# Attention, a gated MLP and a second MLP after layer norm: the norm's factor per token is moved from the second MLP's input to its output

## The chip, the cores and the metric

The kernel runs on one core of one Trainium2 chip. The metric is the device time of the whole program in microseconds (us); lower is better.

## What is computed

Two sequences of 3136 tokens, 256 features, float32 throughout. Cut to what matters:

```python
scores = z @ z.T / S;  x = u * (np.maximum(scores, 0) ** 2 @ v)          # attention, gated by u
h = np.maximum(x @ w_in, 0)                                              # MLP 1, 256 -> 1024
conv = sum(conv_w[k] * shifted(h, k - 1) for k in range(3))              # along the tokens
y = (h * sigmoid(conv)) @ w_out                                          # 1024 -> 256
mu = y.mean(-1, keepdims=True);  var = ((y - mu) ** 2).mean(-1, keepdims=True)
xn = (y - mu) / np.sqrt(var + 1e-6) * g_ln                               # layer norm
out = y + np.maximum(xn @ w_ch1, 0) @ w_ch2                              # MLP 2 and residual
```

## The kernel before, in words

Every float32 product is split into a high and a low part, so that each matrix product is three matmuls on TensorE (PE): high by high, low by high, high by low. Names ending in `h` and `l` are these parts.

Attention runs over 14 chunks of up to 512 tokens; its outputs grow in the PSUM tile `av` and go through DRAM (`gated`) to the MLPs. The MLPs run over 17 blocks of tokens, 15 of three tiles of 128 tokens and two of two tiles, in `mlps(c, when)` (L811). The work of attention for later chunks stands between that of the MLPs. Only the last three blocks have no attention left beside them.

Inside a block, for each of eight slices of the 1024 hidden features: `up` makes hidden values (`hps`, L831 to L833), ScalarE (ACT) and VectorE (DVE) apply relu, convolution and sigmoid and split the result into `gh` and `gl`, and `down` (L847 to L849) adds tile after tile into the accumulator `y`, a PSUM tile of two banks: tiles 0 and 1 lie in the first bank, tile 2 in the second. There is one place for `y`, so the first MLP's output, the second MLP's output and the next block's first MLP follow each other in it. (For the last two blocks the first MLP's accumulator is `av`, the second's a shared `y`, one half each.)

When the first MLP is complete, ACT copies all tiles of the accumulator to SBUF (`ysb`, L932). DVE takes statistics per tile from the copy (`bst`, L937), aggregates them to mean and variance (`mv`, L942) and adds epsilon (`ve`, L949); GpSimd (POOL) raises that to the power −1/2 (`rs`, L953); a Newton step on DVE sharpens it (L960 to L962); DVE writes `xn`, centred and scaled, per tile (L972). PE transposes `xn` into `tps` (L992); ACT and DVE multiply by g and split into `xth` (L1000) and `xtl` (L1005). The second MLP follows: `h2ps`, `g2h` (L1020), `g2l` (L1025), `down` again. At the end one DVE operation adds the accumulator to `ysb` (residual, L1033), and one DMA on SyncE's queue stores the block (L1039).

The order of everything is set ahead of time by a planner (`Program.order`, L154): each operation has the engines it may run on with a price in us, what it reads and writes (by tile of the accumulator), and a due time, `when` or `when2`, from a few constants (`TURN`, `DEFER`). On each engine, among those ready, the earliest due goes first, and the instructions of each engine are then held to that order. The waits on semaphores between engines are not the planner's: they follow from which tile buffers each instruction reads and writes. Where the planner leaves a gap on PE, `fill` (L1136, L1138) puts matmuls on zeros into it, if the accumulator last written has more to come.

The few lines on which this hangs:

```python
key = (o.ways[0][0] != e, o.due, o.n)                # L219: what goes first on engine e
n = int((gaps.get(o, 0.0) - 0.1) / FILL)             # zero matmuls in a planned gap
if n > 0 and not y_used:
    fill(n, wps, True)
elif n > 0 and to_come[last[0]]:
    fill(n, last[1](), False)
```

Of the kernel before, what the change touches and what calls it, by code (L numbers as in the profile page):

```python
# [11 lines left out]
AF = mybir.ActivationFunctionType  # L12
# [3 lines left out]
P = 128  # L16
# [16 lines left out]

UP1, DOWN1, TURN, UP2 = 0.4, 0.14, 0.6, 0.36
LENGTH = 14.0, 14.0, 8.0, 8.0
DEFER = 50.0, 40.0, 0.0
HELP = 1.3
A_PLACES = 4
GH = ("DVE", "ACT")
AH = ("ACT", "DVE")  # L40
CAPS = {"s": 3, "m": 3, "ld": 4}
FUSED = 2, 4, 1
FLOAT = ("ACT", "POOL")
WH = ("ACT", "POOL")
VH = ("ACT", "POOL")
# [45 lines left out]
class Program:  # L91
# [7 lines left out]
    def op(self, ways, fn, reads=(), writes=(), adds=(), takes=(), due=None, late=None, name="", port=False, kb=None):  # L99


        o = Op()
        o.ways, o.fn, o.due, o.late, o.name, o.port, o.kb = ways, fn, due, late, name, port, kb
        o.before, o.after, o.n = set(), [], len(self.ops)
        o.adds, o.spare = tuple(adds), None
        for k in reads:
            assert k in self.writers, (name, k)
            o.before.update(self.writers[k])
            self.readers.setdefault(k, []).append(o)
        for k in writes:  # L110
            o.before.update(self.writers.get(k, ()))
            o.before.update(self.readers.pop(k, ()))
            self.writers[k] = [o]
        for k in adds:
            o.before.update(self.readers.get(k, ()))
            self.writers.setdefault(k, []).append(o)
        o.before.discard(o)
        bufs = []
        for k in (*reads, *writes, *adds, *((t,) for t in takes)):
            if isinstance(k[0], Buf) and k[0] not in bufs:  # L120
                bufs.append(k[0])
        for b in bufs:
            b.users.append(o)
        o.bufs = bufs
        self.ops.append(o)
        return o
# [168 lines left out]
def attn_moe_kernel(ctx: ExitStack, tc: tile.TileContext, zt, ut, v, w_in, conv_w, w_out, g_ln, w1, w2, out):  # L295
# [515 lines left out]
    def mlps(c, when):  # L811
# [115 lines left out]
        def rows(i):  # L927
            return at(y)[:, (i0 + i) * D : (i0 + i + 1) * D]

        op(  # L930
            [("ACT", 0.1 + 0.00078 * n * 2)],
            lambda e: nc.scalar.copy(flat(at(y, "ysb")), flat(at(acc).rearrange("p a b -> p (a b)"))),  # L932
            reads=[(acc, i0 + i) for i in range(ntt)], writes=[(y, i0)], name="ysb",
        )
        for i in range(ntt):
            op(
                [("DVE", 0.328)], lambda e, i=i: nc.vector.bn_stats(at(bst, "bst")[:, i, :], rows(i)),  # L937
                reads=[(y, i0)], writes=[(bst, i)], name="bn",
            )
        for i in range(ntt):  # L940
            op(
                [("DVE", 0.16)], lambda e, i=i: nc.vector.bn_aggr(at(mv, "mv")[:, i, :], at(bst)[:, i, :]),  # L942
                reads=[(bst, i)], writes=[(mv, i)], name="bn",
            )
        def stat():
            return at(ve, "ve")[:, :ntt], at(r, "rs")[:, :ntt], at(q, "rq")[:, :ntt]

        op(
            [("DVE", 0.07)], lambda e: nc.vector.tensor_scalar(stat()[0], at(mv)[:, :ntt, 1], EPS, None, ALU.add),  # L949
            reads=[(mv, i) for i in range(ntt)], writes=[(ve, 0)], name="ve",  # L950
        )
        op(
            [("POOL", 1.285)], lambda e: nc.gpsimd.tensor_tensor(stat()[1], stat()[0], mhalf[:, :ntt], ALU.pow),  # L953
            reads=[(ve, 0)], writes=[(r, 0)], name="pow", port=True,
        )


        def newton(e):
            v_, r_, q_ = stat()
# [2 lines left out]
            nc.vector.scalar_tensor_tensor(r_, q_, 1.5, r_, ALU.add, ALU.mult)  # L962

        op(
            [("DVE", 0.6)], newton, reads=[(ve, 0), (r, 0)], writes=[(r, 1)], takes=[q], name="newton",
        )
        xns = []
        for i in range(ntt):
            xn = buf("xn")
            op(  # L970
                [("DVE", 0.402)],
                lambda e, i=i, xn=xn: nc.vector.tensor_scalar(  # L972
                    at(xn, "xn"), rows(i), at(mv)[:, i, 0:1], at(r)[:, i : i + 1], ALU.subtract, ALU.mult
                ),
                reads=[(y, i0), (mv, i), (r, 1)], writes=[(xn, 0)], name="xn", port=True,
            )
            xns.append(xn)
        if c == NK - 1:
            th, tl = buf("xh", True), buf("xl", True)
        elif tail:  # L980
# [32 lines left out]
        for k in range(NF):  # L1013
            ps = buf("w", kind="m")
            gh, gl = buf("gh", True), buf("gl", True)
            for ways, fn, reads, due, d in up(ps, "w1", k, th, tl, n, when2(TURN + 0.02 + UP2 * k / NF)):
# [21 lines left out]
        dma(  # L1038
            lambda: nc.sync.dma_start(  # L1039
                out=out[s:e_, :].rearrange("(i p) d -> p i d", p=P),  # L1040
                in_=flat(at(y)).rearrange("p (i d) -> p i d", d=D),
            ),
            n, reads=[(y, i0)], due=when2(1.1), name="out",
        )


    def note(*keys):
# [164 lines left out]
```

## Time and profile before

| | |
|---|---|
| median of 3 runs | 1109.61 us (1109.04 to 1109.82) |
| the profiled execution | 1108.97 us |
| its span in the trace | 1107.2 us |
| PE busy | 1093.4 us (99%) |
| DVE busy | 863.4 us (78%) |
| ACT busy | 705.2 us (64%) |
| POOL busy | 31.4 us (3%) |
| clock granted to TensorE, mean | 1.0 |

The span is the part of the execution that the profiler's records cover; the execution's own time is 1.8 us longer. Busy time counts each engine's instructions. Matmuls overlap in the pipeline, so that their recorded lengths add up to more than the time from one start to the next, and a PE that is busy in the table is not PE at its peak: the zero matmuls count as busy too. Before each instruction the trace gives the idle time of its engine and what ended it.

### The profile page before, as it was taken

The page shows a single profiled execution, that of the slowest core. Times are in us where ns is not written, and L with a number is a line of the kernel's source. Part 1 is how long each engine was busy: PE and PEld are TensorE (multiplying, and loading weights), DVE is VectorE, ACT ScalarE, POOL GpSimd, SP SyncE. Part 2 cuts the span into 40 slices and gives each one's busy share as a digit, 9 for nine tenths or more (in the row PEclk, how much of TensorE's full clock was granted, in tenths as well). Part 3 has the DMA queues.
Part 4 walks back from the last instruction along what each step waited for, and adds up shares of the span by engine and source line. Part 5 has one row for each costly group of instructions (what it writes and reads, how often), then busy time and mean ns, then how long its engine had stood idle before and what let it go on. Part 6 is the DMA issues. An engine that isn't in the chain of part 4 may idle for free.

```text
span 1107.2 us, 19228 instructions
## 1 busy us (share of the span) xinstructions
PE 1093.4 (99%) x6674; PEld 1027.3 (93%) x6674; DVE 863.4 (78%) x1828; ACT 705.2 (64%) x1452; POOL 31.4 (3%) x46
## 2 busy tenths in 40 slices
PE   9999999999999999999999999999999999999998
PEld 7777988989999989899989999999899999999998
DVE  7999999987868695969594959595948768478773
ACT  7778887775647575857484857574737547356552
POOL 2000000000000000000000000000000000000000
PEclk9999999999999999999999999999999999999999
DMA  6876887777655431313131413322525635440000
GB/s 201 243 191 156 204 186 175 169 152 161 112 134 89 110 94 43 91 53 94 51 106 46 126 37 79 88 63 58 105 78 97 143 66 97 109 78 27 25 15 20
DMA packets 373778, 115.44 MB, mean 104 GB/s; under 512 B 277296, under 2 KB 365360, under 8 KB 373680
## 3 DMA queue, kind: packets, MB, share of 16 engines
q1 hardware_dynamic: 373680, 114.21, 43.5%
q8 instruction: 52, 0.85, 0.3%
q14 instruction: 46, 0.38, 0.1%
HBM read 64.74 MB, written 46.47 MB: 100 GB/s over the span
## 4 chain that ended last, share of the span: by engine, by line
PE 87%; DVE 4%; DMA 3%; ACT 3%; SPq 2%; issue 1%; POOL 0%; DVEq 0%; ACTq 0%
PE av L746 11%; PE av L749 11%; PE av L748 11%; PE y L847 8%; PE y L849 8%; PE y L848 8%; PE h2ps L831 4%; PE h2ps L832 4%; PE h2ps L833 4%; PE hps L831 4%; PE hps L832 4%; PE hps L833 4%; PE s L704 3%; PE s L705 3%; DMA land<-turned 2%; SPq L651 1%
## 5 line engine op out<-in xcount | busy, mean ns | idle before, releaser
L746 PE MATMUL av<-ah,vh 128*128 128x512 f32 (+2 forms) x700 | 258.6, 369 | 3.2 <-ACT a L722 1.1
L749 PE MATMUL av<-ah,vl 128*128 128x512 f32 (+2 forms) x700 | 256.3, 366 | 0.0
L748 PE MATMUL av<-al,vh 128*128 128x384 f32 (+2 forms) x672 | 247.6, 368 | 2.5 <-DVE al L683 2.0
L1025 DVE SCALAR_TENSOR_TENSOR g2l<-h2ps,g2h 128x384 fp32r<-128x384 f32 (+1 forms) x136 | 73.4, 540 | 114.4 <-ACT g2h L1020 113.4
L1020 ACT ACTIVATE g2h<-h2ps 128x384 fp32r<-128x384 f32 (+1 forms) x136 | 65.3, 480 | 138.8 <-PE h2ps L833 138.1
L746 PEld LDWEIGHTS av<-ah,vh 128*128 128x128 f32 x700 | 131.8, 188 | 17.0 <-ACT ah L394 2.5
L749 PEld LDWEIGHTS av<-ah,vl 128*128 128x128 f32 x700 | 131.7, 188 | 14.3
L748 PEld LDWEIGHTS av<-al,vh 128*128 128x128 f32 x672 | 126.6, 188 | 16.6 <-DVE al L683 6.1
L713 ACT ACTIVATE a<-s 128x512 f32<-128x512 f32 (+2 forms) x196 | 106.2, 557 | 38.2 <-PE s L705 37.6
L683 DVE TENSOR_TENSOR al<-a,ah 128x512 fp32r<-128x512 f32 (+2 forms) x182 | 115.3, 641 | 3.1 <-ACT ah L394 2.1
L683 DVE TENSOR_TENSOR al<-land,ah 128x384 fp32r<-128x384 f32 (+2 forms) x154 | 91.7, 596 | 25.3 <-ACT ah L394 20.9
L847 PE MATMUL y<-woh,gh 128*128 128x256 f32 x392 | 109.9, 280 | 1.1 <-DVE ysb L1033 1.1
L847 PE MATMUL y<-w2h,g2h 128*128 128x256 f32 x392 | 110.0, 281 | 0.2 <-DVE ysb L1033 0.2
L849 PE MATMUL y<-woh,gl 128*128 128x256 f32 x392 | 110.0, 281 | 0.1
L849 PE MATMUL y<-w2h,g2l 128*128 128x256 f32 x392 | 110.0, 281 | 0.0
L848 PE MATMUL y<-w2l,g2h 128*128 128x256 f32 x392 | 109.8, 280 | 0.0
L848 PE MATMUL y<-wol,gh 128*128 128x256 f32 x392 | 109.6, 280 | 0.0
L394 ACT CAST ah<-a 128x512 fp32r<-128x512 f32 (+2 forms) x184 | 105.9, 584 | 4.1 <-PE av L749 1.7
L722 ACT ACTIVATE a<-a 128x512 f32<-128x512 f32 (+2 forms) x183 | 106.8, 594 | 1.6
L626 DVE STREAM_TRANSPOSE bl<-a 128x512 f32<-128x512 f32 (+1 forms) x146 | 94.7, 657 | 9.8 <-ACT a L722 9.2
L394 ACT CAST ah<-land 128x384 fp32r<-128x384 f32 (+2 forms) x136 | 73.8, 546 | 34.7 <-DMA land<-turned 16.7
L882 DVE SCALAR_TENSOR_TENSOR t<-h,cw,t 128x384 f32<-128x384 f32 (+1 forms) x136 | 80.7, 598 | 14.6 <-ACT t L873 14.1
(119 smaller groups left out, 2448.1 us busy)
## 6 DMA issues: line engine op xcount, KB each, us to landing
turned<-bl SPq DMA_DIRECT2D x90, 256.0 KB, 2.5
land<-turned SPq DMA_DIRECT2D x328, 48.0 KB, 2.3
land<-turned SPq DMA_DIRECT2D x168, 56.0 KB, 2.3
turned<-bl SPq DMA_DIRECT2D x44, 192.0 KB, 2.3
land<-turned SPq DMA_DIRECT2D x120, 64.0 KB, 2.5
out_dram<-ysb SPq DMA_DIRECT2D x15, 384.0 KB, 2.7
vst<-in_v_dram SPq DMA_DIRECT2D x11, 512.0 KB, 4.8
x<-gated SPq DMA_DIRECT2D x14, 386.0 KB, 3.9
```

The source lines that it names most:

```text
L394: nc.scalar.copy(dst, src)
L626: [("DVE", price("dve_turn", w))], lambda e: nc.vector.transpose(at(b, "bl")[:, :w], at(ab)[:, :w]),
L683: lambda e: nc.vector.tensor_tensor(at(al, "al")[:, :n], a(), f(at(ah)[:, :n]), ALU.subtract),
L713: [("ACT", price("act_ps", n))], lambda e: nc.scalar.activation(a(), at(ps)[:, :n], AF.Relu),
L722: op([("ACT", price("act", n))], lambda e: nc.scalar.activation(a(), a(), AF.Square), writes=[(ab, 0)], name="square")
L746: nc.tensor.matmul(p, vhj, at(ah)[:, :n], start=first(b, d), stop=False, **kw)
L748: nc.tensor.matmul(p, vhj, at(al)[:, :n], start=False, stop=False, **kw)
L749: nc.tensor.matmul(p, vlj, at(ah)[:, :n], start=False, stop=False, **kw)
L831: nc.tensor.matmul(p, a, h_, start=d == 0, stop=False)
L847: nc.tensor.matmul(p, a, wh, start=first(acc, (i0 + i) // 2), stop=False, **kw)
L848: nc.tensor.matmul(p, a, wl, start=False, stop=False, **kw)
L849: nc.tensor.matmul(p, b, wh, start=False, stop=k == NF - 1, **kw)
```

## The change

The layer norm's factor per token, r, is positive and the second MLP is relu between two linear maps, so r can multiply its output in place of its input. The statistics then read the accumulator in PSUM per tile (L937), and the centred tile is taken from PSUM too, on ACT or DVE (`center`, L951 and L953), with its sign turned (mu − y on ACT is one operation); g is multiplied by −1 once for that (L1085). The copy `ysb` (L962) comes after these in the program, and is now needed by the residual alone. `ve`, power and Newton get due times of their own (`REST`). The residual is a DVE operation per tile, y2 · r + ysb (L1043). The last block's store is two DMAs of one tile each (L1051). `DEFER` for the third last block goes from 50 to 10, so that its second MLP is due earlier. Line numbers in the new kernel's rows are its own: L847 to L849 become L849 to L851, the transposes L1001, fill L1150.

```diff
-DEFER = 50.0, 40.0, 0.0
+DEFER = 10.0, 40.0, 0.0
+CENTER = ("ACT", "DVE")
+REST = 0.9
...
+        def sums1(i, acc=acc):
+            return at(acc).rearrange("p a b -> p (a b)")[:, (i0 + i) * D : (i0 + i + 1) * D]
+
+        for i in range(ntt):
+            op(
+                [("DVE", 0.35)], lambda e, i=i: nc.vector.bn_stats(at(bst, "bst")[:, i, :], sums1(i)),
+                reads=[(acc, i0 + i)], writes=[(bst, i)], name="bn",
+            )
+            op(
+                [("DVE", 0.16)], lambda e, i=i: nc.vector.bn_aggr(at(mv, "mv")[:, i, :], at(bst)[:, i, :]),
+                reads=[(bst, i)], writes=[(mv, i)], name="bn",
+            )
+        xns = []
+        for i in range(ntt):
+            xn = buf("xn")
+
+            def center(e, i=i, xn=xn):
+                mu = at(mv)[:, i, 0:1]
+                if e == "ACT":
+                    nc.scalar.activation(at(xn, "xn"), sums1(i), AF.Identity, bias=mu, scale=-1.0)
+                else:
+                    nc.vector.tensor_scalar(at(xn, "xn"), sums1(i), mu, -1.0, ALU.subtract, ALU.mult)
+
+            op(
+                [(e, price("act_scale" if e == "ACT" else "dve_ps", D)) for e in CENTER], center,
+                reads=[(acc, i0 + i), (mv, i)], writes=[(xn, 0)], name="center",
+            )
+            xns.append(xn)
         op(
             [("ACT", 0.1 + 0.00078 * n * 2)],
             lambda e: nc.scalar.copy(flat(at(y, "ysb")), flat(at(acc).rearrange("p a b -> p (a b)"))),
-            reads=[(acc, i0 + i) for i in range(ntt)], writes=[(y, i0)], name="ysb",
-        )
-        for i in range(ntt):
-            op(
-                [("DVE", 0.328)], lambda e, i=i: nc.vector.bn_stats(at(bst, "bst")[:, i, :], rows(i)),
-                reads=[(y, i0)], writes=[(bst, i)], name="bn",
-            )
...
-            reads=[(mv, i) for i in range(ntt)], writes=[(ve, 0)], name="ve",
+            reads=[(mv, i) for i in range(ntt)], writes=[(ve, 0)], due=when2(REST), name="ve",
...
-            op(
-                [("DVE", 0.402)],
-                lambda e, i=i, xn=xn: nc.vector.tensor_scalar(
-                    at(xn, "xn"), rows(i), at(mv)[:, i, 0:1], at(r)[:, i : i + 1], ALU.subtract, ALU.mult
-                ),
-                reads=[(y, i0), (mv, i), (r, 1)], writes=[(xn, 0)], name="xn", port=True,
-            )
...
-        op(
-            [("DVE", 0.1 + 0.001 * n * 2)],
-            lambda e: nc.vector.tensor_tensor(
-                flat(at(y)), flat(at(acc2).rearrange("p a b -> p (a b)")), flat(at(y)), ALU.add
-            ),
-            reads=[(acc2, i0 + i) for i in range(ntt)], writes=[(y, i0)], name="residual",
-        )
...
+        for i in range(ntt):
+            op(
+                [("DVE", price("dve_3", D))],
+                lambda e, i=i: nc.vector.scalar_tensor_tensor(
+                    rows(i), sums1(i, acc2), at(r)[:, i : i + 1], rows(i), ALU.mult, ALU.add
+                ),
+                reads=[(acc2, i0 + i), (r, 1)], writes=[(y, i0 + i)], name="residual",
+            )
+        for a, b in ((0, 1), (1, ntt)) if c == NK - 1 else ((0, ntt),):
...
+    op([("DVE", 0.07)], lambda e: nc.vector.tensor_scalar(gt, gt, -1.0, None, ALU.mult), writes=[("gt",)], name="gt")
```

Since the planner orders everything anew, the diff doesn't show how instructions move. Three places do, as each engine's list of instructions has them (line, operation, output <- inputs, tile; in brackets what it waits for; x3 counts equal ones).

First place: PE at the end of the second MLP of the fourth block, the last of the eight slices, three tiles of three matmuls. Before:

```order
L847 MATMUL y<-w2h,g2h 128x256 [waits Activation_49]
L848 MATMUL y<-w2l,g2h 128x256
L849 MATMUL y<-w2h,g2l 128x256 [waits DVE_49]
L847 MATMUL y<-w2h,g2h 128x256
L848 MATMUL y<-w2l,g2h 128x256
L849 MATMUL y<-w2h,g2l 128x256
L847 MATMUL y<-w2h,g2h 128x256
L848 MATMUL y<-w2l,g2h 128x256
L849 MATMUL y<-w2h,g2l 128x256
L704 MATMUL s<-hl 128x512
```

After:

```order
L849 MATMUL y<-w2h,g2h 128x256 [waits Activation_49]
L850 MATMUL y<-w2l,g2h 128x256
L851 MATMUL y<-w2h,g2l 128x256 [waits DVE_49]
L849 MATMUL y<-w2h,g2h 128x256
L850 MATMUL y<-w2l,g2h 128x256
L851 MATMUL y<-w2h,g2l 128x256
L849 MATMUL y<-w2h,g2h 128x256 [waits DVE_49]
L850 MATMUL y<-w2l,g2h 128x256
L851 MATMUL y<-w2h,g2l 128x256
L748 MATMUL av<-ah,vh 128x512
```

The third tile's first matmul has gained a wait for DVE. On DVE at the same place the list after reads:

```order
L1034 SCALAR_TENSOR_TENSOR g2l<-h2ps,g2h 128x384 [waits Activation_49] x4
L400 CAST gh<-t 128x384 [waits DVE_49,PE_49]
L1043 SCALAR_TENSOR_TENSOR ysb<-y,rs,ysb 128x256 [waits PE_49]
L915 TENSOR_TENSOR gl<-t,gh 128x384 [waits DVE_49]
L1043 SCALAR_TENSOR_TENSOR ysb<-y,rs,ysb 128x256 [waits PE_49]
L1043 SCALAR_TENSOR_TENSOR ysb<-y,rs,ysb 128x256
L915 TENSOR_TENSOR gl<-t,gh 128x384 [waits Activation_49]
```

Three residuals stand where one of 768 columns stood. The first waits for PE's last matmul on tile 1, the second for PE's on tile 2.

Second place: DVE between the end of the first MLP of the sixth block and its statistics. Before:

```order
L683 TENSOR_TENSOR al<-a,ah 128x512 [waits DVE_49]
L937 BN_STATS bst<-ysb 128x6 [waits Activation_49]
L937 BN_STATS bst<-ysb 128x6 x2
L942 BN_AGGR mv<-bst 128x2 [waits DVE_49] x3
L683 TENSOR_TENSOR al<-land,ah 128x512
L949 TENSOR_SCALAR ve<-mv 128x3 [waits DVE_49]
```

After:

```order
L685 TENSOR_TENSOR al<-a,ah 128x512 [waits Activation_49]
L937 BN_STATS bst<-y 128x6 [waits PE_49]
L937 BN_STATS bst<-y 128x6
L937 BN_STATS bst<-y 128x6 [waits Activation_49]
L941 BN_AGGR mv<-bst 128x2 [waits DVE_49] x3
L685 TENSOR_TENSOR al<-a,ah 128x512
L685 TENSOR_TENSOR al<-land,ah 128x512 [waits DMAHW2_49,DMAHW1_49,DMAHW3_49,DMAHW0_49,Activation_49]
```

Before, the statistics wait for ACT's copy once and read the copy. After, the first two read PSUM when PE is done, and the third waits for ACT. On ACT there the list after reads:

```order
L396 CAST ah<-a 128x512 [waits Activation_49]
L962 COPY ysb<-y 128x768 [waits DMAHW1_49,DVE_49,PE_49]
L396 CAST ah<-land 128x512 [waits DMAHW2_49,DMAHW3_49,DMAHW1_49,DMAHW0_49]
L951 ACTIVATE xn<-y,mv 128x256 [waits DVE_49] x3
L869 ACTIVATE h<-hps 128x386 [waits PE_49]
L875 ACTIVATE t<-h,cw 128x384 [waits Activation_49]
```

The copy waits for DVE and stands ahead of the three centring passes. PE's list after, from there to the transposes (six attention matmuls more stand ahead of the first row, back to the end of the accumulator):

```order
L748 MATMUL av<-ah,vh 128x512
L750 MATMUL av<-al,vh 128x512
L751 MATMUL av<-ah,vl 128x512
L833 MATMUL hps<-xh,wih 128x386
L834 MATMUL hps<-xl,wih 128x386
L835 MATMUL hps<-xh,wil 128x386
L748 MATMUL av<-ah,vh 128x512
L750 MATMUL av<-al,vh 128x512 [waits DVE_49]
L751 MATMUL av<-ah,vl 128x512
L1001 MATMUL tps<-ident,xn 128x128 [waits Activation_49] x3
L1001 MATMUL tps<-ident,xn 128x128 x3
```

Third place: PE in the tail, the first MLP of the last blocks. Before:

```order
L849 MATMUL y<-woh,gl 128x256 [waits DVE_49]
L847 MATMUL y<-woh,gh 128x256
L848 MATMUL y<-wol,gh 128x256
L849 MATMUL y<-woh,gl 128x256
L1138 MATMUL y<-zero 128x256 x30
L847 MATMUL y<-woh,gh 128x256 [waits Activation_49]
L848 MATMUL y<-wol,gh 128x256
L849 MATMUL y<-woh,gl 128x256 [waits DVE_49]
```

After, the only such run left in the tail but one of 2:

```order
L834 MATMUL h2ps<-hl,w1h 128x256
L835 MATMUL h2ps<-hl,w1l 128x256
L833 MATMUL h2ps<-hl,w1h 128x256
L834 MATMUL h2ps<-hl,w1h 128x256
L835 MATMUL h2ps<-hl,w1l 128x256
L1150 MATMUL y<-zero 128x256 x6
L849 MATMUL y<-woh,gh 128x256 [waits Activation_49]
L850 MATMUL y<-wol,gh 128x256
L851 MATMUL y<-woh,gl 128x256 [waits DVE_49]
```

The run of 30 zero matmuls is 6 now, and over the whole program 69 after the warm-up have become 17.

## Rows read from the trace of the kernel before

**Rows 1.** The page, parts 1 and 2: busy times; granted clock in 40 slices.
```profile
PE 1093.4 (99%) x6674; PEld 1027.3 (93%) x6674; DVE 863.4 (78%) x1828; ACT 705.2 (64%) x1452; POOL 31.4 (3%) x46
...
PEclk9999999999999999999999999999999999999999
```

**Rows 2.** Windows: stretch, its us, busy us and count by engine, clock, DMA share, GB/s.
```profile
204.00:325.00 121.00, 118.72 (x742) 114.60 (x741) 97.37 (x210) 73.42 (x155) 1.87 (x3) 1.00 0.69 144
...
1024.50:1053.00 28.50, 28.39 (x234) 27.92 (x235) 21.78 (x67) 15.29 (x41) 1.56 (x3) 1.00 0.08 24
```

**Rows 3.** The chain of waits, longest pieces: start, us, engine, tile, line.
```profile
1040.73 3.59 PE y L1138 x30
```

**Rows 4.** Timeline at 1023 us: start, us, engine, line, operation, idle before.
```profile
1023.21 0.28 PE L849 MATMUL y<-w2h,g2l 128*128 128x256 f32 x1
1023.52 0.96 DVE L1033 TENSOR_TENSOR ysb<-y,ysb 128x768 f32<-128x768 f32 x1 [1.17 <-PE y L849]
...
1024.53 0.39 PE L847 MATMUL y<-woh,gh 128*128 128x256 f32 x1 [1.05 <-DVE ysb L1033]
```

**Rows 5.** Timeline, PE, from the sixth block's first-MLP end to its transposes.
```profile
517.57 0.28 PE L849 MATMUL y<-woh,gl 128*128 128x256 f32 x1
...
517.68 0.39 PE L746 MATMUL av<-ah,vh 128*128 128x512 f32 x1
...
517.91 0.40 PE L748 MATMUL av<-al,vh 128*128 128x512 f32 x1
...
528.16 0.82 PE L992 MATMUL tps<-ident,xn 128*128 128x128 f32 x6
```

**Rows 6.** Timeline at 1091 us, the two last blocks.
```profile
1091.39 0.68 DVE L1033 TENSOR_TENSOR ysb<-y,ysb 128x512 f32<-128x512 f32 x1
...
1092.22 0.36 PE L847 MATMUL y<-w2h,g2h 128*128 128x256 f32 x1 [0.20 <-DVE ysb L1033]
```

**Rows 7.** One tile (xh, xl): duration ns min/median/max, first and last start, forms.
```profile
L1000 ACT ACTIVATE xh<-tps,gt x2: 474/475/476, 1086.9 to 1088.5; 128x256 fp32r<-128x256 f32 x2
L1005 DVE SCALAR_TENSOR_TENSOR xl<-tps,gt,xh x2: 484/484/485, 1087.4 to 1089.0; 128x256 fp32r<-128x256 f32 x2
```

**Rows 8.** Groups by line and form, DVE: busy us, mean ns, idle before and its releasers.
```profile
L913 DVE TENSOR_TENSOR gl<-t,gh 128x384 fp32r<-128x384 f32 x120 | 66.1, 552 | 3.1 <-ACT gh L394 0.3
...
L937 DVE BATCH_NORM_STATS2 bst<-ysb 128x6 f32<-128x256 f32 x49 | 17.8, 414 | 13.0 <-ACT ysb L932 12.9
L972 DVE TENSOR_SCALAR xn<-ysb,mv,rs 128x256 f32<-128x256 f32 x49 | 17.4, 408 | 0.1
L1005 DVE SCALAR_TENSOR_TENSOR xtl<-tps,gt,xth 128x384 fp32r<-128x384 f32 x30 | 17.2, 609 | 4.2 <-ACT xth L1000 4.2
...
L1033 DVE TENSOR_TENSOR ysb<-y,ysb 128x768 f32<-128x768 f32 x15 | 14.3, 957 | 4.8 <-PE y L849 4.8
...
L942 DVE BATCH_NORM_AGGREGATE mv<-bst 128x2 f32<-128x6 f32 x49 | 5.2, 157 | 0.0
```

**Rows 9.** Groups by line and form, ACT.
```profile
L1000 ACT ACTIVATE xth<-tps,gt 128x384 fp32r<-128x384 f32 x30 | 16.0, 579 | 2.7 <-PE tps L992 2.7
...
L932 ACT COPY ysb<-y 128x768 f32<-128x768 f32 x15 | 12.0, 803 | 20.0 <-PE y L849 20.0
```

**Rows 10.** Timeline of the end.
```profile
1102.40 0.28 PE L849 MATMUL y<-w2h,g2l 128*128 128x256 f32 x1
1102.72 0.69 DVE L1033 TENSOR_TENSOR ysb<-y,ysb 128x512 f32<-128x512 f32 x1 [0.84 <-PE y L849]
```

**Rows 11.** DMA issues: queue, count, KB each, median us to landing.
```profile
lh<-hl SPq DMA_DIRECT2D x10, 128.0 KB, 2.3
...
out_dram<-ysb SPq DMA_DIRECT2D x2, 256.0 KB, 3.2
```

**Rows 12.** The page's part 5: busy, mean ns, idle before and its releaser.
```profile
L746 PE MATMUL av<-ah,vh 128*128 128x512 f32 (+2 forms) x700 | 258.6, 369 | 3.2 <-ACT a L722 1.1
...
L748 PE MATMUL av<-al,vh 128*128 128x384 f32 (+2 forms) x672 | 247.6, 368 | 2.5 <-DVE al L683 2.0
```

More of the change, by code (lines that the diff above doesn't have):

```diff
@@ L928, in rows @@
             return at(y)[:, (i0 + i) * D : (i0 + i + 1) * D]
-        op(
-            [("ACT", 0.1 + 0.00078 * n * 2)],
-            lambda e: nc.scalar.copy(flat(at(y, "ysb")), flat(at(acc).rearrange("p a b -> p (a b)"))),
-            reads=[(acc, i0 + i) for i in range(ntt)], writes=[(y, i0)], name="ysb",
-        )
+        def sums1(i, acc=acc):
+            return at(acc).rearrange("p a b -> p (a b)")[:, (i0 + i) * D : (i0 + i + 1) * D]
         for i in range(ntt):
             op(
-                [("DVE", 0.328)], lambda e, i=i: nc.vector.bn_stats(at(bst, "bst")[:, i, :], rows(i)),
-                reads=[(y, i0)], writes=[(bst, i)], name="bn",
+                [("DVE", 0.35)], lambda e, i=i: nc.vector.bn_stats(at(bst, "bst")[:, i, :], sums1(i)),
+                reads=[(acc, i0 + i)], writes=[(bst, i)], name="bn",
             )
-        for i in range(ntt):
             op(
@@ L944, in mlps @@
             )
+        xns = []
[13 more added lines that the diff above has]
+        op(
+            [("ACT", 0.1 + 0.00078 * n * 2)],
+            lambda e: nc.scalar.copy(flat(at(y, "ysb")), flat(at(acc).rearrange("p a b -> p (a b)"))),
+            reads=[(acc, i0 + i) for i in range(ntt)], writes=[(y, i0 + i) for i in range(ntt)], name="ysb",
+        )
         def stat():
@@ L953, in mlps @@
             [("POOL", 1.285)], lambda e: nc.gpsimd.tensor_tensor(stat()[1], stat()[0], mhalf[:, :ntt], ALU.pow),
-            reads=[(ve, 0)], writes=[(r, 0)], name="pow", port=True,
+            reads=[(ve, 0)], writes=[(r, 0)], due=when2(REST), name="pow", port=True,
         )
@@ L964, in mlps @@
         op(
-            [("DVE", 0.6)], newton, reads=[(ve, 0), (r, 0)], writes=[(r, 1)], takes=[q], name="newton",
+            [("DVE", 0.6)], newton, reads=[(ve, 0), (r, 0)], writes=[(r, 1)], takes=[q], due=when2(REST), name="newton",
         )
-        xns = []
-        for i in range(ntt):
-            xn = buf("xn")
-            op(
-                [("DVE", 0.402)],
-                lambda e, i=i, xn=xn: nc.vector.tensor_scalar(
-                    at(xn, "xn"), rows(i), at(mv)[:, i, 0:1], at(r)[:, i : i + 1], ALU.subtract, ALU.mult
-                ),
-                reads=[(y, i0), (mv, i), (r, 1)], writes=[(xn, 0)], name="xn", port=True,
-            )
-            xns.append(xn)
         if c == NK - 1:
@@ L1030, in mlps @@
             down(acc2, "w2", k, gh, gl, when2(TURN + 0.02 + UP2 * k / NF + 0.06))
-        op(
-            [("DVE", 0.1 + 0.001 * n * 2)],
-            lambda e: nc.vector.tensor_tensor(
-                flat(at(y)), flat(at(acc2).rearrange("p a b -> p (a b)")), flat(at(y)), ALU.add
-            ),
-            reads=[(acc2, i0 + i) for i in range(ntt)], writes=[(y, i0)], name="residual",
-        )
[L1038 to L1043, printed above, removed]
-        )
+        for i in range(ntt):
[7 more added lines that the diff above has]
+        for a, b in ((0, 1), (1, ntt)) if c == NK - 1 else ((0, ntt),):
+            dma(
+                lambda a=a, b=b: nc.sync.dma_start(
+                    out=out[s + a * P : s + b * P, :].rearrange("(i p) d -> p i d", p=P),
+                    in_=flat(at(y)).rearrange("p (i d) -> p i d", d=D)[:, a:b, :],
+                ),
+                128 * (b - a), reads=[(y, i0 + i) for i in range(a, b)], due=when2(1.1), name="out",
+            )
     def note(*keys):
```

## The prediction

> **What bounds the kernel now.** Read the page's busy times first [rows 1]: TensorE (PE) is busy for 1093.4 of a 1107.2 us span, and its clock row stands at 9 in all forty slices, so what it loses is lost to waits and to filling matmuls, not to the clock. The windows by stretch [rows 2] show where another engine comes near: from 204 to 325 us VectorE (DVE) is busy for 97.37 of 121 us, in the tail from 1024.5 to 1053 us for 21.78 of 28.5. The chain of waits shows what PE does there that is no work: one run of 30 zero matmuls, 3.59 us [rows 3], which the kernel puts into a planned gap. There are 69 of them after the warm-up. The timeline of a hand-off [rows 4] then gives the price of the one thing that the change multiplies: PE's last matmul of a block starts at 1023.21, DVE's residual runs from 1023.52 for 0.96 us, PE goes on at 1024.53. A matmul of 256 columns takes 0.11 us from start to start [rows 5], so PE lost 1024.53 − 1023.32 = 1.21 us for an operation of 0.96: a trip from PE to DVE and back costs **0.24 us and the operation**. Another timeline [rows 6] shows that such a wait goes by the whole PSUM tile: at 1092.22 PE's first matmul of the last block waits for the residual of the block before it, which reads the other half of the tile. PE was idle for it (0.20 us of idle are put down to that releaser).
>
> **A. Stops inside an accumulation.** Before, DVE's residual and ScalarE's (ACT's) copy come when an accumulator is whole. After, DVE reads tile 0 when PE has ended tile 1, and PE's first matmul on tile 2 waits for that read: the third `y<-w2h,g2h` row of the order shows the wait, which the row of before lacks. The order of the whole program has 21 such places: 10 with a residual and 4 with a statistics operation where nothing stands between, 7 where three to six attention matmuls do (0.23 us each [rows 5], 0.7 to 1.4 us, enough to hide one trip). A residual of 256 columns is a three-operand DVE operation with a pointer scalar from PSUM; its nearest row is 0.484 us [rows 7]. The statistics operation is 0.414 from SBUF [rows 8]. So 10 × (0.24 + 0.48) + 4 × (0.24 + 0.41) = 7.2 + 2.6 = 9.8 us. Two residuals in place of one at the second last block add some 0.3: **+10.1**. It can't be less than the operations alone, 14 × 0.414 = 5.8, since the read waits for a matmul and the next matmul for the read; if DVE is one operation late at each (gl, 0.552 [rows 8]) it is 14 × 0.55 = 7.7 more, 17.8.
>
> The Trainium skill (PSUM — Partial Sum Buffer, PSUM bank collisions raise a hardware error) asks for a guard by bank and quadrant, not by address; tile 2 lies in another bank than tile 0, so by it these stops are not needed, and the sum would lose A. The row at 1092.22 and the order's wait speak for a guard by tile.
>
> **B. The chain from the first MLP's output to the transposes.** Before, the transposes of the sixth block start at 528.16, when its last first-MLP matmul started at 517.57 [rows 5]: 10.6 us, in which copy, statistics, power, Newton and scaling all fit. After, power and Newton are off this path, and the planner moves the transposes up: between the two, the order leaves 12 attention matmuls and 3 of 386 columns for the sixth block, 12 × 0.23 + 3 × 0.18 (at the same pace per column) = 3.3 us, and 2.0 to 4.0 us in 14 blocks, 2.93 in the mean. The chain that has to fit: DVE's statistics of tile 2 wait for ACT's copy of the same accumulator in 12 blocks (the order's `[waits Activation_49]`). One statistics operation 0.41, the copy 0.80 [rows 9], another statistics operation 0.41, three aggregates 0.30 (0.157 each, overlapping), three centring passes: nearest ACT row 0.475 [rows 7], some 0.09 less to the next of a row, 1.23; and five hand-overs of 0.04 (0.03 and 0.05 in [rows 4]): 0.41 + 0.80 + 0.41 + 0.30 + 1.23 + 0.20 = 3.35 us. That is 3.35 − 2.93 = 0.42 over the mean cover, 12 times: **+5.0**. Without the copy in it the chain is 2.5 us and hidden nearly everywhere: 0. With both engines one operation of 0.6 us late it is 12 × (0.42 + 0.6) = 12.2.
>
> **C. The tail's own chains.** In the third last block the second MLP now follows its transposes at once: xth 0.579 [rows 9] and the low part 0.609 [rows 8] stand bare but for some matmuls, 1.0. The last block has 1.4 us of cover for a chain of 2.4: 1.0. **+2.0** (0 to 3).
>
> **D. Zero matmuls.** The order counts 17 after the warm-up where 69 stood: 52 × 0.12 (3.59 over 30) = 6.2 us at most. 19 of them stood around 206 to 222 us, 2.3 us, where DVE paces the work [rows 2] and its operations up to the same place are as many as before: taken 1.1. 28 stood in the tail, 3.4 us, taken 2.2 since DVE is near there too [rows 2]; five elsewhere 0.6. **−3.9** (0 to −6.2).
>
> **E, F, G.** The hand-off at 1023 goes, as six matmuls of the next block stand before the next write: **−1.2** (0 to −1.2). The end: PE's last matmul starts at 1102.40, the residual of 0.69 follows [rows 10]; two of 0.48 with 0.09 overlap are 0.2 longer, and the last store is half as large: 256 KB took 3.2 us to land, 128 KB (another transfer) 2.3 [rows 11]. **−0.3** (+0.3 to −0.7). Where PE stands, ACT and DVE catch up, so that stops which stood before (5.7 us in the two largest groups [rows 12]) shrink: **−1.5** (0 to −3). DVE itself loses 42 scaling passes of 0.408 [rows 8] and has about 8 us more for the finer residuals (49 × 0.484 where 15 × 0.957 and 2 × 0.687 stood); not being the bound, this is costed at nothing. So is the doubled sign on the factor g (one operation of two columns, behind others in the load phase).
>
> The Trainium skill (Perfetto Trace Analysis, Optimizing Scalar/DVE Operations) gives DVE some 65 ns more per instruction on PSUM than on SBUF. As an estimate by that page, the two statistics passes in B's chain and the four in A would add about 2 us. No row here has this operation on PSUM, and the sum goes without.
>
> **Sum:** 10.1 + 5.0 + 2.0 − 3.9 − 1.2 − 0.3 − 1.5 = **+10.2 us** on the profiled execution's 1108.97, 1119.2. The median of the runs, 1109.61, stands 0.64 above that execution, so 1119.8 for the median.
>
> **The rivals.**
> 1. Only the stops inside accumulations cost; the chain of B is hidden, since the copy comes late enough: 10.2 − 5.0 = +5.2, 1114.8. For it: the planner meant it so. Against: the order's waits on ACT.
> 2. DVE is late at each stop, because residual and statistics stand behind other operations: 10.2 + 7.7 = +17.9, 1127.5. For it: `gh` and `gl` stand around the residual in the order. Against: DVE is at 78% [rows 1].
> 3. Faster: the stops cost the operations alone (5.8), the chains fit their cover, and all zero matmuls go for good: 5.8 − 6.2 − 1.2 − 0.3 − 1.5 = −3.4, 1106.2. It decides where a trip costs no more than its operation and the chain stays under 2.9 us.
> 4. The change doesn't act as the order reads: the waits at tile 2 are met when PE comes to them, as a guard by bank would make them (A is 0): 10.2 − 10.1 = +0.1, 1109.7, no change. For it: nothing in the rows but the small 0.20 of [rows 6].
>
> **How the numbers follow.** About 0.2%, 2.2 us, can be told from no change. My forecast (1115.5 to 1126) 0.55, rival 1 0.13, rival 2 0.09, rival 3 0.12, rival 4 0.11. Slower is the forecast with rivals 1 and 2: 0.77; same 0.11; faster 0.12. The range reaches from just below rival 3 (1106.2) to above rival 2 (1127.5) by the 3 us of G's bounds: 1105.5 to 1130.5. Outside are some 0.07 below and 0.06 above it, where the chains of B are late as well.
>
> **What would show it.** A: some 14 new waits of PE on DVE of about 0.7 us at `y<-w2h,g2h` and `y<-woh,gh`. B: waits of PE at the transposes, released by ACT's or DVE's centring, of 0.2 to 1 us in most blocks, with the copy between two statistics operations. D: a shorter run of zero matmuls in the tail. It is wrong if PE's idle time grows by less than 8 us.

## The result, and the profile after

The changed kernel takes 1124.49 us (median of four runs, 1123.68 to 1124.70) against 1109.71 before: a ratio of 1.0132, 95% interval 1.0114 to 1.0149. It is 14.8 us slower. Forecast were 1119.8 us and slower, with a range to 1130.5. The profiled execution took 1124.70 us.

The page after, its span and busy times (engine, busy us, share, instructions):

```profile
span 1122.9 us, 19110 instructions
...
PE 1097.2 (98%) x6622; PEld 1021.9 (91%) x6622; DVE 864.8 (77%) x1829; ACT 718.5 (64%) x1482; POOL 32.1 (3%) x48
```

PE does 52 matmuls less than in [rows 1], and its share of the span falls from 99% to 98%. DVE is as busy as before, ACT has 13 us more, for the centring passes above all. No engine has become the bound; PE waits. For what, the list of PE's waits says (line, releaser: us in total, times, longest):

```profile
PE y L849 <- DVE ysb L1043: 6.8, 12, 0.7
...
PE y L849 <- DVE bst L937: 2.1, 4, 0.5
...
PE tps L1001 <- ACT xn L951: 1.5, 4, 0.8
PE tps L1001 <- ACT h L869: 1.4, 2, 0.9
...
PE tps L1001 <- DVE xn L953: 0.8, 4, 0.2
...
PE av L748 <- ACT ah L396: 1.6, 1, 1.6
```

Twelve waits for a residual and four for a statistics operation, none over 0.7 us: the stops of part A, where in the kernel before two waits for a residual stood:

```profile
PE y L847 <- DVE ysb L1033: 1.2, 2, 1.1
```

One of the twelve, in the timeline of the fifth block (start, us, engine, line, operation, idle before):

```profile
494.06 0.28 PE L851 MATMUL y<-w2h,g2l 128*128 128x256 f32 x1
494.37 0.48 DVE L1043 SCALAR_TENSOR_TENSOR ysb<-y,rs,ysb 128x256 f32<-128x256 f32 x1 [0.18 <-PE y L851]
...
494.91 0.38 PE L849 MATMUL y<-w2h,g2h 128*128 128x256 f32 x1 [0.58 <-DVE ysb L1043]
...
495.13 0.28 PE L850 MATMUL y<-w2l,g2h 128*128 128x256 f32 x1
...
495.25 0.28 PE L851 MATMUL y<-w2h,g2l 128*128 128x256 f32 x1
```

PE's last matmul on the second tile starts at 494.06. The residual of the first tile starts as soon as it is done, 494.37, and takes 0.48, as forecast. PE's next matmul, on the third tile, starts at 494.91, where 494.18 was due: 0.73 us, and all ten bare stops with a residual (bare: no other matmul stands in between) lie within 0.01 us of that. What the forecast missed stands in the next two rows: from the first matmul after the stop to the second are 0.22 us, and 0.12 from there on. The first is 0.1 us slow to hand over to its successor. The hand-off in [rows 4] has this too: its 1024.53 lasts 0.39 where 1023.21 lasts 0.28.

The chain of part B, at the eleventh block:

```profile
807.33 0.76 DVE L937 BATCH_NORM_STATS2 bst<-y 128x6 f32<-128x256 f32 x2 [0.67 <-PE y L851]
...
808.18 0.80 ACT L962 COPY ysb<-y 128x768 f32<-128x768 f32 x1 [1.15 <-DVE bst L937]
...
809.01 0.43 DVE L937 BATCH_NORM_STATS2 bst<-y 128x6 f32<-128x256 f32 x1 [0.92 <-ACT ysb L962]
...
809.36 0.30 DVE L941 BATCH_NORM_AGGREGATE mv<-bst 128x2 f32<-128x6 f32 x3
...
809.56 1.20 ACT L951 ACTIVATE xn<-y,mv 128x256 f32<-128x256 f32 x3 [0.58 <-DVE mv L941]
...
810.09 1.39 PE L1001 MATMUL tps<-ident,xn 128*128 128x128 f32 x6
```

The copy sits between the second and the third statistics operation and holds the third back until 809.01, by 0.92 us of idle time. The six transposes take 1.39 us from their start, in [rows 5] they took 0.82.

The wait for the copy has a second price, which the forecast did not have. In the tenth block the low part of an attention operand (`al`) stands behind the statistics on DVE, and PE waits for it:

```profile
751.71 0.76 DVE L937 BATCH_NORM_STATS2 bst<-y 128x6 f32<-128x256 f32 x2 [0.87 <-ACT ysb L962]
...
752.39 0.67 DVE L685 TENSOR_TENSOR al<-a,ah 128x512 fp32r<-128x512 f32 x1
...
753.12 0.50 PE L750 MATMUL av<-al,vh 128*128 128x512 f32 x1 [0.59 <-DVE al L685]
```

DVE is idle for 0.87 us until the copy is done, and PE then for 0.59.

The end, with the last store in two pieces:

```profile
1118.38 0.28 PE L851 MATMUL y<-w2h,g2l 128*128 128x256 f32 x1
1118.70 0.88 DVE L1043 SCALAR_TENSOR_TENSOR ysb<-y,rs,ysb 128x256 f32<-128x256 f32 x2 [0.83 <-PE y L851]
1119.24 0.82 SPq L1050 DMA_DIRECT2D out_dram<-ysb  x2
```

From PE's last matmul to the end of the span are now 1122.9 − 1118.38 = 4.5 us, before 1107.2 − 1102.40 = 4.8 [rows 10].

**An account of PE's time.** Undisturbed, a matmul is followed by the next after 0.0022 us and 0.000449 us per column (0.117 us for 256 columns, 0.232 for 512, as in [rows 5]). Summed over the trace, what two starts lie further apart than that is time lost, by what stands at the place:

| us lost | accumulator, waits over 0.15 | around transposes | all the rest | total | zero matmuls in all |
|---|---|---|---|---|---|
| before | 2.0 | 4.2 | 20.1 | 26.3 | 128 |
| after | 12.0 | 11.6 | 25.0 | 48.6 | 76 |
| change | +10.0 | +7.4 | +4.9 | +22.3 | −52 × 0.117 = −6.1 |

22.3 − 6.1 − 0.3 at the end = 15.9 us, against 15.7 between the two profiled executions. Most of the 4.2 us around the transposes in the row of before is no wait: six transposes come out some 0.2 us over this rule wherever nothing holds them up.

### The profile page after: what moved, and what is told of

Read it like the earlier page. It is cut to its first block, busy times and chain, and to the rows that moved or that the text cites. A ratio compares the mean times of both kernels' runs of the same rounds, so it can differ in the third digit from the quotient of the medians.

```text
span 1122.9 us, 19110 instructions
## 1 busy us (share of the span) xinstructions
PE 1097.2 (98%) x6622; PEld 1021.9 (91%) x6622; DVE 864.8 (77%) x1829; ACT 718.5 (64%) x1482; POOL 32.1 (3%) x48
## 4 chain that ended last, share of the span: by engine, by line
PE 83%; DVE 6%; ACT 4%; DMA 4%; issue 1%; SPq 1%; DVEq 0%; POOL 0%; ACTq 0%
PE av L751 10%; PE av L748 10%; PE av L750 10%; PE y L849 8%; PE y L851 8%; PE y L850 8%; PE h2ps L833 4%; PE h2ps L834 4%; PE h2ps L835 4%; PE hps L833 4%; PE hps L834 4%; PE hps L835 4%; PE s L706 3%; PE s L707 3%; DMA land<-turned 2%
## 5 line engine op out<-in xcount | busy, mean ns | idle before, releaser
L849 PE MATMUL y<-w2h,g2h 128*128 128x256 f32 x392 | 111.3, 284 | 6.8 <-DVE ysb L1043 6.8
L849 PE MATMUL y<-woh,gh 128*128 128x256 f32 x392 | 110.8, 283 | 2.1 <-DVE bst L937 2.1
L851 PE MATMUL y<-w2h,g2l 128*128 128x256 f32 x392 | 109.7, 280 | 0.0
L851 PE MATMUL y<-woh,gl 128*128 128x256 f32 x392 | 109.7, 280 | 0.0
L899 ACT ACTIVATE t<-t 128x384 f32<-128x384 f32 (+1 forms) x136 | 69.0, 510 | 51.5 <-DVE t L892 51.2
L869 ACT ACTIVATE h<-hps 128x386 f32<-128x386 f32 (+1 forms) x136 | 65.0, 481 | 47.7 <-PE hps L835 46.7
```

The source lines that it names most:

```text
L849: nc.tensor.matmul(p, a, wh, start=first(acc, (i0 + i) // 2), stop=False, **kw)
L851: nc.tensor.matmul(p, b, wh, start=False, stop=k == NF - 1, **kw)
```

## The experiments

The theory: the stops inside an accumulation and the copy in the chain before the transposes are what costs, each on its own. The rivals: the new plan is worse as such; or the waits only show where time would be lost in any case.

**1. Reads of whole accumulators only.** Statistics and residuals are planned when all tiles are done.

```diff
 lambda e, i=i: nc.vector.bn_stats(at(bst, "bst")[:, i, :], sums1(i)),
-reads=[(acc, i0 + i)], writes=[(bst, i)], name="bn",
+reads=[(acc, i0 + x) for x in range(ntt)], writes=[(bst, i)], name="bn",
...
-reads=[(acc2, i0 + i), (r, 1)], writes=[(y, i0 + i)], name="residual",
+reads=[(acc2, i0 + x) for x in range(ntt)] + [(r, 1)], writes=[(y, i0 + i)], name="residual",
```

> The changed kernel, but statistics and residuals are planned only when the whole accumulator is done, so no read stands between two tiles of one accumulation. Theory (stops): its trace shows 14 bare stops, each 0.68 to 0.74 us late at the next matmul and some 0.11 more before the second one, so 14 x 0.84 = 11.8 us should go. 16 zero matmuls come back (1.9 us, partly in place of other stops). Chain from accumulator to transposes: the statistics start later but the planned cover grows too, so it stays within 4 us either way. 1124.5 - 11.8 + 1 = 1113.7 (1110 to 1117). Rival (the new plan as such is worse: fewer zero matmuls, transposes too early, clock): the stops only show time that would be lost elsewhere, and it stays at 1122 to 1126.

Measured: 1103.77 us, 0.9943 of before (0.9926 to 0.9960). It is faster than both kernels, and by 20.7 us faster than the change, where 11 were expected: below the range given. In the account the accumulator's waits fall from 12.0 to 0.8 us, as expected, and the transposes' from 11.6 to 5.3, which was not: the planner, which starts the statistics later, also leaves more work of PE before the transposes (3.4 us in the mean by the list of instructions, where the change leaves 2.8). This run takes both losses away, so it doesn't tell them apart.

**2. The copy after the centred tiles.**

```diff
-reads=[(acc, i0 + i) for i in range(ntt)], writes=[(y, i0 + i) for i in range(ntt)], name="ysb",
+reads=[(acc, i0 + i) for i in range(ntt)] + [(x, 0) for x in xns], writes=[(y, i0 + i) for i in range(ntt)], name="ysb",
```

> The changed kernel, but the copy of the accumulator to SBUF is held back until the centred tiles are written, so that it no longer stands between two statistics operations. The stops inside accumulations stay (all but one). Theory (chain): in the trace of the changed kernel the matmul pitches around the transposes lose 11.6 us against 4.2 before; about two thirds of the 7.4 more is the copy's 0.80 us in the chain, so 4 to 5 us go and 12 zero matmuls (1.4 us) come back: 1124.5 - 4.5 + 1 = 1121 (1119 to 1123). Rival 1 (the copy is not in the way, the chain is long because the centring passes and the statistics share one PSUM tile): no change, 1124 to 1125. Rival 2 (the copy, moved back, keeps the accumulator longer and the next accumulation waits for it): slower, 1126 and more.

Measured: 1114.42 us, 1.0043 of before (1.0029 to 1.0057), 10 us less than the change. The stops stay (11.9 us in the account). Around the transposes 4.5 us are lost where it was 11.6, which is the level of before. 7 us come from there, so the copy was all of that loss, not two thirds of it; in front of attention's matmuls with `al` and `ah` 4 us less are lost. The time is below the range given. The plan moved in this run too.

**3. Both edits.**

> Both edits: reads only of whole accumulators, and the copy after the centred tiles. Theory: both losses go, 1124.5 - 11.8 - 5 + 1.1 (9 zero matmuls) = 1109 (1106 to 1112). If the two losses overlap (a stop gives the chain time), less: 1112 to 1114. Rival (plan as such): 1120 and more.

Measured: 1100.55 us, 0.9915 of before (0.9899 to 0.9932): 24 us less than the change, and below the range given. The two edits alone give 20.7 + 10.1 = 30.8, so 7 us of them are the same time. By the account most of that is at the transposes, where each edit alone takes away 6 to 7 us.

**4. The finer residual in the kernel before, alone.** Three additions per block, one per tile, in place of one of 768 columns. Nothing else of the change. (The planner is also told of the copy's output and the store's input by tile; these two lines are not shown.)

```diff
-op([("DVE", 0.1 + 0.001 * n * 2)], lambda e: nc.vector.tensor_tensor(
-    flat(at(y)), flat(at(acc2).rearrange("p a b -> p (a b)")), flat(at(y)), ALU.add),
-    reads=[(acc2, i0 + i) for i in range(ntt)], writes=[(y, i0)], name="residual")
+for i in range(ntt):
+    op([("DVE", price("dve_3", D))], lambda e, i=i: nc.vector.tensor_tensor(
+        rows(i), at(acc2).rearrange("p a b -> p (a b)")[:, (i0 + i) * D : (i0 + i + 1) * D], rows(i), ALU.add),
+        reads=[(acc2, i0 + i)], writes=[(y, i0 + i)], name="residual")
```

> The kernel before, with one edit: the residual of each block is three additions of 256 columns in place of one of 768, each planned when its own tile is done. Nothing else of the change. Theory (stops): the list of instructions has 12 bare stops of PE's third tile behind the first addition; an addition of 256 columns is about 0.42 us by the two lengths seen (0.957 for 768, 0.687 for 512), so a stop is 0.24 + 0.42 + 0.11 for the second matmul = 0.77, and 12 x 0.77 = 9.2 us: 1109.7 + 9.2 = 1119 (1116 to 1121). Rival (a finer residual ends earlier, so the next accumulator starts earlier, and the stop hides in the pipeline): 1107 to 1110.

Measured: 1119.74 us, 1.0088 of before (1.0069 to 1.0107), 10.0 us slower than the 1109.7 of before. Its trace at one stop:

```profile
550.95 0.28 PE L849 MATMUL y<-w2h,g2l 128*128 128x256 f32 x1
551.27 0.42 DVE L1034 TENSOR_TENSOR ysb<-y,ysb 128x256 f32<-128x256 f32 x1 [0.46 <-PE y L849]
...
551.75 0.39 PE L847 MATMUL y<-w2h,g2h 128*128 128x256 f32 x1 [0.52 <-DVE ysb L1034]
```

The addition takes 0.42 us, and PE is 0.69 late (551.75 − 551.06). So the rival falls: a finer residual alone, in a kernel that is otherwise as before, brings the stops and their price.

**5. The change with two tile buffers.** The accumulator `y` becomes two tiles of one bank each; the plan is the change's, instruction for instruction, but for the copy in two pieces.

```diff
+def two(name):
+    return tuple(psum.tile([P, 2 * D], F32, tag="y" + x, name=name, bufs=1) for x in "ab")
+tags["y"] = 1, two
...
-lambda e: nc.scalar.copy(flat(at(y, "ysb")), flat(at(acc).rearrange("p a b -> p (a b)"))),
+lambda e: [
+    nc.scalar.copy(at(y, "ysb")[:, a:b], cols(at(acc), a, b))
+    for a, b in ((i0 * D, (i0 + 2) * D), ((i0 + 2) * D, (i0 + ntt) * D)) if b > a
+],
```

> The changed kernel with the plan it has, instruction for instruction, but the accumulator y is two tile buffers, one per bank (tiles 0 and 1 in one, tile 2 in the other; the copy becomes two, of 512 and 256 columns). The list of instructions loses all bare stops, since the third tile's matmul no longer writes the buffer that DVE reads. Theory (a stop is the wait by whole tile buffer): 14 x 0.84 = 11.8 us go; the copy, now in two pieces, is 0.2 longer in the chain of most blocks, +2: 1124.5 - 11.8 + 2 = 1114.7 (1112 to 1117). Rival 1 (a matmul beside a read of the other bank is held up in hardware all the same): 1122 and more. Rival 2 (what made the run with whole reads 20 us faster was its own plan, with later transposes, and the stops are worth less than they show): 1119 to 1122.

Measured: 1104.97 us, 0.9962 of before (0.9948 to 0.9977): 19.5 us less than the change with the same plan. This is the run that decides, since each engine's operations stand in the order of the change. The same stop as above, in its timeline:

```profile
487.44 0.28 PE L861 MATMUL y<-w2h,g2l 128*128 128x256 f32 x1
...
487.56 0.28 PE L859 MATMUL y<-w2h,g2h 128*128 128x256 f32 x1
...
487.67 0.28 PE L860 MATMUL y<-w2l,g2h 128*128 128x256 f32 x1
...
487.76 0.48 DVE L1056 SCALAR_TENSOR_TENSOR ysb<-y,rs,ysb 128x256 f32<-128x256 f32 x1 [0.17 <-PE y L861]
487.78 0.28 PE L861 MATMUL y<-w2h,g2l 128*128 128x256 f32 x1
...
487.90 0.34 PE L843 MATMUL hps<-xh,wih 128*128 128x386 f32 x1
```

The residual starts at 487.76, and PE, on the other buffer, keeps its pace of 0.11 us through it. Here the Trainium skill (PSUM — Partial Sum Buffer, PSUM bank collisions raise a hardware error), which asks for a guard by bank and quadrant, is borne out: a read of one bank beside matmuls into the other ran without a stop. The stops of the change came from the guard by whole tile buffer. Both rivals of this run fall. But it gave 19.5 us where 10 were expected, below the range given. In the account (28.4 us lost, 20.2 less than the change) 11.8 went at the accumulator, as the theory has it, and 3.0 around the transposes. Since PE's order is the same in both runs, the other 5.4 can be compared matmul by matmul: 1.9 are the slow second matmuls after a stop, 2.5 stood in front of matmuls that need `al`, and 1 is spread. PE's waits say the same: for `al` 3.2 us in the change, and here

```profile
PE av L760 <- DVE al L695: 1.3, 5, 0.5
```

**6. The same and the late copy.**

> The changed kernel with the copy held back until after the centred tiles and with two tile buffers; reads are planned as early as the change plans them. Against the run with two buffers alone (1105.0) only the copy's place differs. Theory (the copy in the chain before the transposes costs on its own): in the trace with two buffers the pitches around the transposes lose 8.6 us, in the two runs with a late copy 4.5 to 4.8, so 4 us go: 1101 (1099 to 1103). Rival (the copy only cost because stops stood beside it): 1104 to 1106.

Measured: 1101.51 us, 0.9936 of before (0.9921 to 0.9951), 3.5 us less than in 5. Around the transposes 4.5 us are lost, 8.6 in 5. At the block whose chain is shown above:

```profile
796.43 1.09 DVE L947 BATCH_NORM_STATS2 bst<-y 128x6 f32<-128x256 f32 x3 [0.31 <-PE y L861]
...
797.44 0.30 DVE L951 BATCH_NORM_AGGREGATE mv<-bst 128x2 f32<-128x6 f32 x3
...
797.64 1.21 ACT L961 ACTIVATE xn<-y,mv 128x256 f32<-128x256 f32 x3 [1.26 <-DVE mv L951]
...
799.13 0.88 ACT L973 COPY ysb<-y 128x512 f32<-128x512 f32 x2
...
799.38 0.82 PE L1014 MATMUL tps<-ident,xn 128*128 128x128 f32 x6
```

The three statistics run on without a gap, the centring follows, the copy comes last, and the transposes take 0.82 us again. The rival falls. The copy in the chain costs, then, some 3.5 us without stops beside it; with the stops, in experiment 2, it was 10, of them 7 around the transposes. In both the planner also moved other work.

**7. Two tile buffers and both edits.**

> Both edits (whole reads, copy after the centred tiles) and two tile buffers on top. Theory: there are no stops left for the two buffers to take away, the chain's reads on ACT and DVE can overlap where they touch different buffers, and the copy is longer: within 2 us of the run with both edits, 1100.5 (1098.5 to 1102.5). Rival (reads kept apart by tile buffer still cost in the chain): 1097 and less.

Measured: 1099.20 us, 0.9910 of before (0.9895 to 0.9925). It is within the range given, and its interval and that of 3 overlap. It is the fastest of the study, 10.5 us under the kernel before and 25 under the change.

**8. Two tile buffers for the finer residual of 4.**

> The kernel before with three additions per residual, as in the run that took 1119.7, and with two tile buffers; the plan is the same, instruction for instruction, but for the copy in two pieces. Theory (a stop is the wait by whole tile buffer, in any plan): the 12 bare stops go, 12 x 0.84 = 10.1 us and what hangs on them (their removal in the changed kernel gave 19.5 for 14 stops, so up to 16 here), and the hand-off at 1023 us shortens: 1119.7 - 11 = 1108.5 (1104 to 1110). Rival (additions by tile cost DVE more than they show): 1114 and more.

Measured: 1108.93 us, 1.0002 of before (0.9992 to 1.0012). That is 10.8 us less than in 4 and the time of the kernel before: what the finer residual had cost is gone, and nothing is gained beyond: 14 stops of two kinds in one plan, 12 of one kind in the other, both go when the third tile has its own buffer.

**9. The kernel before without its zero matmuls.** The 69 after the warm-up are left out.

```diff
-        elif n > 0 and to_come[last[0]]:
-            fill(n, last[1](), False)
```

> The kernel before without its 69 zero matmuls after the warm-up (the 59 of the warm-up stay). Term D of the prediction counted a zero matmul at 0.12 us where nothing else is late, and at half to two thirds of that in the two stretches with most of them, so 69 x 0.075 = 5 us should go: 1104.5 (1102 to 1107). Rival 1 (they stand only where PE would wait anyway): 1108.5 to 1110. Rival 2 (PE that idles there is granted a lower clock): slower, 1111 and more, with a granted clock under 1 in those windows.

Measured: 1109.97 us, 1.0007 of before (0.9998 to 1.0017): no change. 69 × 0.12 = 8.3 us of work are gone and none of the time. Where the 30 stood, PE's waits and the windows of the trace show why (waits as above; a window's us, busy us and count of PE, its weight loads, DVE, ACT and POOL, granted clock):

```profile
PE y L847 <- ACT gh L394: 2.1, 1, 2.1
PE y L849 <- DVE gl L913: 1.3, 1, 1.3
```

```profile
1036.00:1043.00 7.00, 3.60 (x25) 2.98 (x25) 7.00 (x21) 6.12 (x18) 0.00 (x0) 1.00 0.01 1
1043.00:1050.00 7.00, 7.00 (x48) 7.00 (x47) 4.52 (x16) 2.78 (x7) 0.00 (x0) 0.76 0.00 0
1050.00:1060.00 10.00, 10.00 (x76) 9.90 (x76) 9.20 (x29) 8.12 (x23) 0.86 (x1) 1.00 0.01 2
```

PE now waits 2.1 us for ACT and 1.3 for DVE, 3.4 of the 3.59 us that the zero matmuls took. DVE is busy through the whole window from 1036 to 1043, PE for 3.60 of its 7 us. After it, PE is granted 0.76 of the clock for 7 us, a mean between the two levels of 1.2 and 2.4 GHz. In [rows 1] the clock stands at 9 throughout. So rival 1 of this run holds, with a small part of rival 2: the zeros stand where PE would wait, and they keep the clock. The granted clock of the whole run says so too: 0.996 to 0.998 in the ten executions of this kernel, 0.998 to 1.000 in the thirteen of before beside them.

**10. The due time of the third last block as before.**

```diff
-DEFER = 10.0, 40.0, 0.0
+DEFER = 50.0, 40.0, 0.0
```

> The changed kernel with the due time of the third last block's second MLP as before (50 in place of 10), so only the tail is planned otherwise; the list is the same up to it. Theory: term C (the tail's own chains; in the trace of the changed kernel the matmul pitches from 1052 to 1057 lose 2.6 us at the transposes and behind them) goes, 16 zero matmuls come back, 1.9 us at most: 1123 to 1125.5. Rival (the tail is where the change loses): 1116 to 1120.

Measured: 1124.48 us, 1.0145 of before (1.0125 to 1.0164), the time of the change itself. 16 zero matmuls came back and the time lost fell from 48.6 to 45.7, which nearly cancels. The tail is not where the change loses.

## Why the prediction was right, and where its sizes were off

The direction, the two mechanisms and most of the places were right. The size was not: the terms gave 10.2 us, the account 15.9. Part by part:

- **A and E** (stops, and the hand-off that goes): 10.1 − 1.2 = 8.9 forecast, 10.0 measured at the accumulator. The counts were exact: ten bare stops of 0.73 to 0.74 with a residual, four of 0.68 with a statistics operation, where 0.72 and 0.65 were forecast. The seven behind attention matmuls showed nothing over 0.2 us but one at 974 us (0.5). Left out was what comes with a stop: the slow second matmul, 0.1 us each and 1.9 in all, which [rows 4] already hinted at.
- **B and C**: 7.0 forecast, 7.4 measured around the transposes, but by luck in the sum: B was 3.3 where 5.0 were forecast, C 4.0 where 2.0 were. Of the transposes of blocks 2 to 14 those of only five blocks (2, 3, 9, 11 and 14) are late, by 0.5 to 1.4 us, where the forecast had most blocks; in the tenth the wait stood elsewhere, at 753.12 above. The mechanism of B is shown by experiments 2 and 6: with the copy out of the chain, the loss is that of before. In C, the transposes of the third last block lose 1.9 us, to waits for ACT's relu (`h`, L869, in the list above) and not for xth and its low part as forecast.
- **D**: −3.9 forecast, −6.1 by the account, and they stayed gone. Experiment 5 has the same 76 zero matmuls, and what it loses apart from accumulator and transposes is 28.4 − 0.2 − 8.6 = 19.6 us, no more than the 20.1 of before; so that the change loses 25.0 there is not the price of the missing zero matmuls. Pricing them one by one is not borne out either: in the order of before, taking them out is worth nothing (experiment 9). The stretch where D was halved, since DVE paces the work there, reads in the change

```profile
225.00:230.00 5.00, 3.26 (x17) 2.80 (x16) 3.05 (x8) 1.27 (x3) 0.00 (x0) 0.95 0.61 111
230.00:240.00 10.00, 10.00 (x55) 10.00 (x55) 7.01 (x16) 5.24 (x11) 0.00 (x0) 0.85 0.85 194
240.00:250.00 10.00, 8.78 (x52) 8.15 (x51) 9.91 (x22) 7.82 (x18) 0.00 (x0) 1.00 0.75 151
```

  The clock of 0.85 after 230 us is not there in [rows 2]. It costs little that lasts: experiment 10 has the same order here and a clock of 1.00, and three of its matmuls start at 227.84, 229.36 and 233.68 us that start here at 229.20, 231.67 and 235.04. PE falls behind by 1.0 us more and has it back, since it waits in 10 for what it comes late to here.
- **F**: −0.3 forecast and measured.
- **G** is the step that failed: −1.5 forecast, because ACT and DVE would catch up while PE stands. They stood too. DVE's idle time before statistics and residuals was 13.0 [rows 8] and 4.8 [rows 8] + 0.8 [rows 10] = 18.6 us, and is 22.7 + 14.8 = 37.5 (the last rows of this section). PE's waits in the page's two groups did not shrink from 5.7 us, they grew by 1.0, those for `al` from 2.5 [rows 12] to 3.5:

```profile
L748 PE MATMUL av<-ah,vh 128*128 128x512 f32 (+2 forms) x700 | 258.6, 369 | 3.2 <-ACT ah L396 1.6
...
L750 PE MATMUL av<-al,vh 128*128 128x384 f32 (+2 forms) x672 | 248.5, 370 | 3.5 <-DVE al L685 3.2
```

  All the rest of the account grew by 4.9 us, and in experiment 5 4.4 us of second matmuls and waits for `al` went with the stops.

So the forecast was 5.7 us short: 6.4 in G and in what comes with a stop, 1.1 in A and E and 0.4 in B and C, less 2.2 in D. That D erred the other way is luck.

The rivals: 1 (the chain hidden) fell by the 3.3 us of B. 2 (DVE late at each stop, 1127.5) came nearer to the 1124.5 measured than the forecast of 1119.8, and is wrong in mechanism: DVE started its residual 0.31 us after the start of the matmul that it waited for, as soon as that was done. 3 had D in full, as the account has it, but needed stops that cost the operations alone, and each cost 0.68 to 0.74 us. 4, a guard by bank, is not what this program does, and experiment 5 made it so: it is worth 19.5 us. The 65 ns more for DVE on PSUM that the Trainium skill gives (Perfetto Trace Analysis, Optimizing Scalar/DVE Operations) came out as follows (groups of after by line and form: busy us, mean ns, idle before):

```profile
L937 DVE BATCH_NORM_STATS2 bst<-y 128x6 f32<-128x256 f32 x49 | 19.8, 426 | 22.7 <-PE y L851 13.1 <-ACT ysb L962 9.1 <-ACT xn L951 0.4
...
L953 DVE TENSOR_SCALAR xn<-y,mv 128x256 f32<-128x256 f32 x7 | 3.4, 482 | 2.1 <-ACT xn L951 2.1
...
L1043 DVE SCALAR_TENSOR_TENSOR ysb<-y,rs,ysb 128x256 f32<-128x256 f32 x49 | 22.1, 481 | 14.8 <-PE y L851 14.5
```

The statistics take 426 ns from PSUM against 414 from SBUF [rows 8], 12 more; the pass that writes `xn` 482 against 408, 74 more, but with one pointer scalar in place of two. That figure of the Trainium skill is engine-busy time, of which it says that profiled latency is about twice as long; so these lengths don't test it closely. The second lies near it, the first far under it.

## What to carry to other kernels

An accumulator that several engines read by parts while PE still adds to it should be as many tile buffers as it has banks, or be read only when whole: the guard goes by buffer, and each read between two tiles of one buffer costs PE a trip to the reader and back, 0.7 us and more here, whatever the planner believes. Before counting removed filler work as a gain, look at what the engine would wait for there: it was worth nothing in experiment 9, where the order stayed, and stayed gone in full by the account of experiment 5, where the order had moved. An engine that waits for another is not free to catch up: look at what stands behind it. When something is taken off a chain, look at what else reads the same buffer: a copy that nobody needs yet can still stand in the way of one that is needed.

## What the runs showed that was not expected

- After a stop, PE's second matmul comes 0.22 us after its first, 0.1 more than the pace, in the rows at 494 us.
- In two places the granted clock fell behind a stretch in which PE was less busy: 0.76 over 7 us behind a stretch with 3.60 us busy of 7, 0.85 over 10 us behind one with 3.26 of 5. At the second place, experiments 5 and 10, with the same order, had 1.00.
- With the same plan, taking away 14 bare stops that show 10.1 us (10 × 0.74 + 4 × 0.68) gave 19.5 us. 11.8 of it are waits at the accumulator (the 14 with five others), 3.0 stood around the transposes, 2.5 in front of matmuls on `al` and 1.9 in the slow second matmuls. How much of the 3.0 and the 2.5 is due to the copy's guard, which is by buffer too, was not tried apart.
